# Reordering the products of a seven-product block multiplication in a mixture-of-experts layer: (1,2) before (0,3)

## Chip, cores, metric

One core of one Trainium2 chip. The metric is device time in microseconds (us) of one execution; lower is better.

## The reference

Attention (4 batches, 8 heads, 768 positions) makes `x` (3072 x 512). Then comes a mixture of 8 experts with fixed mixing weights `P`, 3072 x 8, from a Sinkhorn iteration:

```python
    for e in range(E):
        h = np.maximum(x @ w1[e], 0.0)
        ye = h @ w2[e]
        out += P[:, e:e + 1] * ye
```

The change touches `x @ w1[e]` of experts 1 to 7 only.

## The kernel before

Experts 1 to 7 work on six chunks of 512 tokens. Each (expert, chunk) of layer 1 is a 2 x 2 block product with seven products instead of eight, once per half `g` of the output columns: 14 products named `(g, k)`. I call one (expert, chunk) a **round**; the layer 1 of the very first one is plain, so there are 41 rounds. Layer 2 of the chunk before runs interleaved: a round has seven slots, each with two layer-1 products (4 matmuls each) and one layer-2 product (8 matmuls).

```python
        def copy(g, name, bank):          # ScalarE: PSUM -> SBUF, one buffer per name
            R[name] = mp.tile([128, 2, 256], F32, tag=f"R{name}", bufs=1, name=f"R{name}")
            nc.scalar.activation(out=R[name], in_=banks[g, bank], func=AF.Copy, bias=0.0, scale=1.0)
        ...
        def relu_sum(g, i, n, bank, name):   # VectorE: h = relu(bank + R[name])
            nc.vector._custom_dve(TENSOR_ADD_SAT, out=block(g, i, n), in0=banks[g, bank],
                                  in1=R[name], s0=65504.0, s1=0.0)

        def step(g, k):
            if k == 1:
                product(g, 1, "y", first=True)
                copy(g, "1", "y")
            if k == 2:
                product(g, 2, "z", first=True, last=True)
                relu_sum(g, 0, 0, "z", "1")
            if k == 6:
                product(g, 6, "y")
                copy(g, "2", "y")
            if k == 5:
                product(g, 5, "w", first=True)
                copy(g, "5", "w")
            if k == 7:
                product(g, 7, "y")
                relu_sum(g, 1, 1, "y", "5")
            if k == 3:
                product(g, 3, "w", last=True)
                relu_sum(g, 0, 1, "w", "2")
            ...                               # k == 4: product into y, relu on ScalarE

        for pair in (((0, 1), (0, 2)), ((0, 5), (0, 6)), ((0, 3), (1, 1)), ((0, 7), (1, 2)),
                     ((1, 5), (1, 6)), ((0, 4), (1, 7)), ((1, 3), (1, 4))):
            for g, k in pair:
                step(g, k)
            yield
```

The comments are added here. The banks y, z, w are PSUM banks out of a pool of four. Product (0,3) adds into w and so must wait until ScalarE has copied w after (0,5); (1,7) adds into y and must wait for the copy of y after (1,6).

The accumulators of expert 0 are weighted by `P` on ScalarE while expert 1 runs, 24 instructions in all.

```python
    def weight_first(c):
        for nb in range(4 * c, 4 * c + 4):
            nc.scalar.activation(out=acc_of(nb), in_=acc_of(nb), func=AF.Copy,
                                 bias=0.0, scale=Pne[:, nb, 0:1])
            yield
    ...
    def body(n):
        ...
        for slot in range(7):
            go("l1", 2 if n == 0 and slot == 0 else 1)
            if slot in (1, 5):
                go("w")
                go("x", 2)
            go("l2")
            if slot in (2, 3, 5, 6):
                go("first")
            ...
    with tc.manual_schedule(engines={mybir.EngineType.DVE}):
        for n in range(len(works)):
            body(n)
```

Part of layer 2 is added into the accumulators by an accumulating DMA from a tile `add` with three buffers. Only VectorE keeps the program's order; the scheduler orders the other engines, and it pulls the weightings of all six chunks into the first rounds.

The softmax here doesn't subtract the row's maximum and nothing guards it: scores larger than these inputs give would overflow.

## Time and profile before

| | |
|---|---|
| time, median of 3 runs | 700.89 us (700.46 to 701.01) |
| span of the profiled run | 699.1 us |
| first layer-1 product of round 1 to the end of the last matmul ("stage") | 184.31 to 694.995, 510.68 us |
| round 1, round 2 | 13.92, 12.83 us |
| every other round from 3 to 40 | 12.23 us |

A round's length is the distance between the starts of its product (0,1) and that of the next round in the timeline. Gaps below are distances between matmul starts less 0.109 us, the usual distance.

The page of before, engines' busy time and the chain that ended last:

```profile
PE 683.9 (98%) x6913; PEld 568.7 (81%) x6913; DVE 570.9 (82%) x1149; ACT 419.8 (60%) x775; POOL 151.4 (22%) x183
...
PE 92%; ACT 4%; DVE 2%; issue 1%; POOL 0%; ACTq 0%
```

The windows view of before: rounds 1 to 3 and one stretch of 100 us later. The first number after the window is its length, then each engine's busy time.

```profile
core 0: us, PE busy (x) PEld busy (x) DVE busy (x) ACT busy (x) POOL busy (x), PEclk, DMA share, GB/s
184.31:198.23 13.92, 12.58 (x114) 10.92 (x113) 10.93 (x22) 13.92 (x28) 1.30 (x2) 1.00 0.27 46
198.23:211.05 12.82, 12.58 (x114) 10.93 (x112) 11.88 (x24) 11.34 (x22) 2.59 (x4) 1.00 0.35 61
211.05:223.28 12.23, 12.23 (x115) 10.96 (x112) 12.04 (x25) 6.98 (x14) 2.54 (x4) 1.00 0.38 66
300.00:400.00 100.00, 100.00 (x918) 89.63 (x917) 86.83 (x160) 55.64 (x114) 22.77 (x27) 1.00 0.53 88
```

From round 3 to round 40, PE never stops. The Trainium skill, "Perfetto Trace Analysis", section "Identifying the Most-Contended Engine", warns that matmul busy time is not a good measure of the distance to the roofline; what shows saturation here is that the starts come every 0.109 us without a gap. In round 1 ScalarE is busy for all of the 13.92 us. In round 3 VectorE is busy 12.04 of 12.23 us.

The timeline of before in round 1 (start, duration, engine, line, operation, tiles, count, idle time and its releaser). Source line 718 is a layer-1 product, 727 the copies R, 733 the relu sums, 641 the weightings.

```profile
188.15 0.64 ACT L727 ACTIVATE R_3541<-l1w 128x512 f32<-128x512 f32 x1
188.63 0.65 ACT L727 ACTIVATE R_3547<-l1y 128x512 f32<-128x512 f32 x1
188.84 0.60 PE L718 MATMUL l1w<-xT_77,S_1_3450 128*128 128x256 f16 x4 [0.85 <-ACT R_3541 L727]
189.11 1.39 ACT L641 ACTIVATE acc_81<-acc_81,Pne 128x512 f32<-128x512 f32 x2
...
193.97 0.66 ACT L727 ACTIVATE R_3618<-l1w 128x512 f32<-128x512 f32 x1
...
194.45 0.67 ACT L727 ACTIVATE R_3624<-l1y 128x512 f32<-128x512 f32 x1
...
195.17 0.60 PE L718 MATMUL l1y<-T_1_3466,S_1_3450 128*128 128x256 f16 x4 [0.50 <-ACT R_3624 L727]
```

The product at 188.84 is (0,3): it waits for the copy of w, which stands behind weightings on ScalarE. The product at 195.17 is (1,7): it waits for the copy R2 of (1,6). By distances between starts the gaps are 1.01 and 0.66 us; the brackets are smaller (0.85 and 0.50) because a modelled matmul end lies later than the next start could. Round 2 has three gaps, of 0.12, 0.40 and 0.09 us, at 200.53, 202.24 and 208.00.

The timeline of before in round 3, which is typical of rounds 3 to 5:

```profile
218.28 0.68 DVE L733 CUSTOM_DVE_ANT_0 hT_3_3872<-l1y,R_3902 128x512 f16<-128x512 f32 x1
...
218.88 0.68 DVE L733 CUSTOM_DVE_ANT_0 hT_3_3872<-l1z,R_3935 128x512 f16<-128x512 f32 x1
...
219.08 0.60 ACT L727 ACTIVATE R_3980<-l1w 128x512 f32<-128x512 f32 x1
...
219.57 0.60 ACT L727 ACTIVATE R_3986<-l1y 128x512 f32<-128x512 f32 x1
...
220.22 0.60 PE L718 MATMUL l1y<-T_3_3730,S_1_3450 128*128 128x256 f16 x4
```

VectorE sums (0,7), then as the fourth of the round's six sums (1,2). ScalarE copies R5 and then R2 (219.57), and (1,7) follows at 220.22, 0.05 us after the copy's end, yet without a gap behind the product before it. So R2's copy has no slack in this round.

### The profile page before, as it was taken

The numbers are of one execution on the slowest core, as the hardware profiler recorded it, in microseconds if no ns is written. First come the engines' busy times: TensorE is split into PE (matmuls) and PEld (weight loads), VectorE is DVE, ScalarE is ACT, GpSimd is POOL, SyncE is SP. The second block draws the span as 40 slices with busy tenths as digits, with TensorE's granted clock in tenths as the row PEclk, the third lists the DMA queues.
The fourth block names the chain that finished last, engine by engine and source line by source line (L and its number), as shares of the span: only waits on it lengthen the run. The fifth ranks groups of instructions, "written<-read, shape, count | busy, mean of one in ns | idle before, by whom it ended". The sixth has DMA issues, their size and how long they took to land.

```text
span 699.1 us, 17004 instructions
## 1 busy us (share of the span) xinstructions
PE 683.9 (98%) x6913; PEld 568.7 (81%) x6913; DVE 570.9 (82%) x1149; ACT 419.8 (60%) x775; POOL 151.4 (22%) x183
## 2 busy tenths in 40 slices
PE   6999999999999999999999999999999999999997
PEld 3666666666588888888888888888888888888885
DVE  7785765757889988888888878988898788988785
ACT  6777676774896554655555565555556555555651
POOL 7432220000012131212212121122212212121210
PEclk8999999999999999999999999999999999999999
DMA  9999591000734287346824594349533964245776
GB/s 180 183 192 129 48 77 17 2 1 2 121 60 76 49 128 129 63 76 110 147 48 75 91 153 77 61 68 164 88 62 61 144 114 77 46 76 108 143 158 153
DMA packets 84256, 65.62 MB, mean 94 GB/s; under 512 B 48336, under 2 KB 64720, under 8 KB 84176
## 3 DMA queue, kind: packets, MB, share of 16 engines
q0 software_dynamic: 74976, 57.17, 58.5%
q1 hardware_dynamic: 7552, 6.30, 3.8%
q10 hardware_dynamic: 1648, 1.05, 0.6%
q8 instruction: 54, 0.88, 0.5%
q14 instruction: 26, 0.21, 0.1%
HBM read 52.45 MB, written 6.29 MB: 84 GB/s over the span
## 4 chain that ended last, share of the span: by engine, by line
PE 92%; ACT 4%; DVE 2%; issue 1%; POOL 0%; ACTq 0%
PE l1y L718 20%; PE l2y L783 20%; PE l1w L718 10%; PE l2w L783 10%; PE l1z L718 5%; PE l2z L783 5%; PE l1b L698 1%; ACT acc_81 L641 0%; PE l_3312 L375 0%; PE l_3246 L375 0%; PE l_1684 L375 0%; PE l_1568 L375 0%; ACT PT_1_0_0_318 L463 0%; PE last_10658 L835 0%; PE last_10646 L835 0%
## 5 line engine op out<-in xcount | busy, mean ns | idle before, releaser
L797 ACT ACTIVATE add<-l2z,Pne 128x256 f32<-128x256 f32 x80 | 33.6, 472 | 77.2 <-PE l2z L783 77.2
L797 ACT ACTIVATE add<-l2w,Pne 128x256 f32<-128x256 f32 x80 | 33.6, 472 | 28.3 <-PE l2w L783 26.5
L797 ACT ACTIVATE add<-l2y,Pne 128x256 f32<-128x256 f32 x80 | 33.7, 473 | 11.6 <-PE l2y L783 9.9
L361 PEld LDWEIGHTS <-w_0_124 128*128 128x128 f16 x384 | 35.4, 98 | 4.0 <-issue 0.2
L805 POOL DMA_DIRECT2D acc_79<-add x21 | 17.7, 844 | 78.4 <-ACT add L797 23.1
L805 POOL DMA_DIRECT2D acc_81<-add x21 | 17.7, 844 | 68.7 <-ACT add L797 29.2
L805 POOL DMA_DIRECT2D acc_80<-add x21 | 17.7, 845 | 67.6 <-ACT add L797 30.0
L805 POOL DMA_DIRECT2D acc_82<-add x21 | 17.8, 847 | 67.0 <-ACT add L797 31.0
L805 POOL DMA_DIRECT2D acc_83<-add x18 | 15.1, 841 | 54.2 <-ACT add L797 22.9
L805 POOL DMA_DIRECT2D acc_84<-add x18 | 15.4, 856 | 45.0 <-ACT add L797 31.8
L800 DVE SCALAR_TENSOR_TENSOR acc_83<-l2y,Pne,acc_83 128x256 f32<-128x256 f32 x44 | 19.2, 477 | 2.9 <-PE l2y L783 2.9
L800 DVE SCALAR_TENSOR_TENSOR acc_79<-l2y,Pne,acc_79 128x256 f32<-128x256 f32 x42 | 18.3, 478 | 3.1 <-PE l2y L783 3.0
L800 DVE SCALAR_TENSOR_TENSOR acc_82<-l2y,Pne,acc_82 128x256 f32<-128x256 f32 x42 | 18.3, 478 | 3.0 <-PE l2y L783 3.0
L800 DVE SCALAR_TENSOR_TENSOR acc_81<-l2y,Pne,acc_81 128x256 f32<-128x256 f32 x42 | 18.3, 477 | 3.0 <-PE l2y L783 3.0
L800 DVE SCALAR_TENSOR_TENSOR acc_80<-l2y,Pne,acc_80 128x256 f32<-128x256 f32 x42 | 18.3, 477 | 2.9 <-PE l2y L783 2.9
L718 PEld LDWEIGHTS <-S_5_6866 128*128 128x128 f16 x192 | 18.8, 98 | 2.2
L718 PEld LDWEIGHTS <-S_2_3728 128*128 128x128 f16 x192 | 18.8, 98 | 2.2
L718 PEld LDWEIGHTS <-S_6_7900 128*128 128x128 f16 x192 | 18.8, 98 | 2.2
L718 PEld LDWEIGHTS <-S_7_8934 128*128 128x128 f16 x192 | 18.8, 98 | 2.2
L718 PEld LDWEIGHTS <-S_3_4798 128*128 128x128 f16 x192 | 18.8, 98 | 2.2
L718 PEld LDWEIGHTS <-S_4_5832 128*128 128x128 f16 x192 | 18.8, 98 | 2.2
L718 PEld LDWEIGHTS <-S_1_3450 128*128 128x128 f16 x160 | 15.6, 98 | 4.1 <-issue 2.1
(2563 smaller groups left out, 2249.1 us busy)
## 6 DMA issues: line engine op xcount, KB each, us to landing
acc_79<-add POOLq DMA_DIRECT2D x21, 256.0 KB, 3.3
acc_80<-add POOLq DMA_DIRECT2D x21, 256.0 KB, 3.3
acc_81<-add POOLq DMA_DIRECT2D x21, 256.0 KB, 3.3
acc_82<-add POOLq DMA_DIRECT2D x21, 256.0 KB, 3.3
acc_83<-add POOLq DMA_DIRECT2D x18, 256.0 KB, 3.4
acc_84<-add POOLq DMA_DIRECT2D x18, 256.0 KB, 10.2
w_0_124<-in_moe_w_dram POOLq DMA_DIRECT2D x1, 1024.0 KB, 12.4
w_0_131<-in_moe_w_dram POOLq DMA_DIRECT2D x1, 1024.0 KB, 18.2
```

Of the source, the lines that this page charges most:

```text
L361: nc.tensor.matmul(out=l1[:, ts(fb % 2, 256)], lhsT=w1[:, dc, ts(fb, 128)], rhs=xT[dc // 2][:, dc % 2, c0:c0 + 256], start=(dc == 0), stop ...
L698: nc.tensor.matmul(out=l1, lhsT=w1[:, dc, ts(fb, 128)], rhs=xT[dc // 2][:, dc % 2, ts(c, CH)], start=(dc == 0), stop=(dc == 3),)
L718: nc.tensor.matmul(out=banks[g, bank][:, f, :], lhsT=lefts1[e][k - 1][:, dc, ts(2 * g + f, 128)], rhs=rights1[c][k - 1][:, dc, :], start=( ...
L783: nc.tensor.matmul(out=banks[bank][q], lhsT=lefts2[e, c][k - 1][:, q, f, :], rhs=rights2[e][k - 1][:, f, :], start=(first and q == 0 and f ...
L797: nc.scalar.activation(out=t[:, q, :], in_=banks[bank][q], func=AF.Copy, bias=0.0, scale=w)
L800: nc.vector.scalar_tensor_tensor(out=dst, in0=banks[bank][q], scalar=w, in1=dst, op0=ALU.mult, op1=ALU.add,)
L805: nc.gpsimd.dma_start(out=acc[c][:, i, n, :, :], in_=t, accum_op=ALU.add)
```

## The change

The intent: give the third slot to (1,1) and (1,2), which need nothing from ScalarE's late copies, and run (0,3) one slot later, when its operands for the sum have long been ready.

```diff
-        for pair in (((0, 1), (0, 2)), ((0, 5), (0, 6)), ((0, 3), (1, 1)), ((0, 7), (1, 2)),
+        for pair in (((0, 1), (0, 2)), ((0, 5), (0, 6)), ((1, 1), (1, 2)), ((0, 7), (0, 3)),
                      ((1, 5), (1, 6)), ((0, 4), (1, 7)), ((1, 3), (1, 4))):
```

The built programs have the same number of instructions on every engine; only their order and their waits differ.

## The prediction

> **What bounds the kernel now.** The page gives PE 683.9 of 699.1 us (98%); the chain that ended last is 92% PE. In the windows from 300 to 600 us PE is busy 100% at a granted clock of 1.00. A busy PE row proves little by itself, so I read starts: in the timeline of one (expert, chunk) round (406.68 to 418.90 us, 12.22 us) a group of 4 matmuls starts every 0.435 us and one of 8 every 0.87, about 109 ns per 256-column matmul. The Trainium skill, "TensorE: Matmul & The Clock Gate", section "Wait — 56ns, not 53.3ns?", gives N / 2.4 GHz + about 2.5 ns, which is 109.2 ns for N = 256; this trace agrees. In 39 of the 41 rounds of the transformed layers PE streams without a gap; no order of products makes that faster.
>
> Gaps exist only in the first two rounds: 1.01 us at 188.84 and 0.40 at 202.24, before product (0,3), which waits for ScalarE's copy of (0,5); 0.66 at 195.17 and 0.09 at 208.00, before (1,7), which waits for the copy of (1,6). About 2.2 us. There ScalarE is busy weighting the accumulators (0.7 us each).
>
> **What the change does.** Nothing is added or removed. In each round (0,3) moves from third to fourth slot, (1,2) from fourth to third; on VectorE their sums change places; ScalarE's copy of (1,1) comes about 0.44 us earlier. The PSUM bank of w stays open a slot longer, but the built program puts the second w into the bank that (1,2)'s sum has freed, at the same place in VectorE's order as before: that sum ends near 412.1, (1,5) starts at 413.67, so no new wait.
>
> **On the critical path.**
> 1. Round 1: (1,1) starts near 187.83, 1.01 us earlier than (0,3) did. But from 188.15 to 195.12 ScalarE works without a gap, on the same work in either order, and (1,7) waits for its last copy. I expect (1,7) at 195.17 as before: gain 0.
> 2. Round 2: 0.40 us gained at 202.24, lost again at (1,7), because VectorE runs back to back from 203.3 to 207.3.
> 3. New dependence: one R2 buffer. The copy of (1,6) must wait until (0,3)'s sum has read the old R2; that sum is now the fifth of the round. In rounds 2 to 5 the fifth sum ends 0.012 us before that copy starts; ScalarE starts about 0.11 us after the VectorE instruction it waits for (R5's copy: 206.74 to 206.86). So the copy comes 0.10 us later, and (1,7), 0.05 us behind it without slack, too: about +0.1 us a round, in 4 rounds: +0.4 us.
> 4. From round 6 on the distance is 0.28 us and (1,7) has 0.12 us of slack: nothing. Last round (distance 0.05): up to +0.06.
>
> Sum: 700.9 + 0.4 = **701.3 us**, 8 in 10 between 700.5 and 702.2. Faster by over 2%: 0.5%; within 2%: 98.5%; slower by over 2%: 1%.
>
> **What would show it.** The waits at 188.84 and 202.24 gone; (1,7) of round 1 still waiting on ScalarE near 195.2, of round 2 near 208.1; rounds 2 to 5 each about 0.1 us longer, from 6 on still 12.22 us.
>
> **What would make it wrong.** ScalarE's chain in round 1 getting shorter (gain up to 1 us); the 0.11 us not paid or absorbed (701.0); the R2 wait reaching the later rounds (0.1 us times 36: 705); bank reuse waiting for another sum than I read.

## The result, and the profile after

After: 701.01 us median of 4 runs (700.53 to 701.64); before, in the same rounds: 700.74 us (700.46 to 701.01). The ratio is 1.0004, 95% interval 0.9987 to 1.0022. A ratio here is the mean time of one kernel's runs over that of the other's in the same rounds, so not quite the ratio of the medians quoted. By time alone nothing can be told. The trace tells more: the stage went from 510.68 to 511.09 us (184.226 to 695.317), 0.41 us longer.

| round | 1 | 2 | 3 | 4 | 5 | 6 | 7 | 8 to 40, each |
|---|---|---|---|---|---|---|---|---|
| before | 13.92 | 12.83 | 12.23 | 12.23 | 12.23 | 12.23 | 12.23 | 12.23 |
| after | 13.90 | 12.92 | 12.32 | 12.32 | 12.33 | 12.23 | 12.27 | 12.23 |

The page of after:

```profile
PE 684.7 (98%) x6913; PEld 568.7 (81%) x6913; DVE 573.6 (82%) x1149; ACT 420.0 (60%) x775; POOL 151.4 (22%) x183
...
PE 91%; ACT 5%; DVE 3%; issue 1%; DMA 1%; ACTq 0%
```

The windows view of after, for the same rounds:

```profile
184.23:198.12 13.89, 12.72 (x113) 10.85 (x112) 10.92 (x22) 13.89 (x28) 1.30 (x2) 1.00 0.27 46
198.12:211.05 12.93, 12.51 (x115) 10.87 (x113) 11.88 (x24) 11.26 (x22) 2.60 (x4) 1.00 0.35 61
211.05:223.37 12.32, 12.32 (x115) 10.94 (x113) 12.03 (x25) 7.07 (x14) 2.54 (x4) 1.00 0.38 66
300.00:400.00 100.00, 100.00 (x918) 89.62 (x917) 87.58 (x159) 55.81 (x115) 22.76 (x27) 1.00 0.54 88
```

Round 3 is 0.09 us longer although PE still counts as busy in all of it: a wait of 0.1 us disappears in the modelled matmul ends. Only starts show it.

The timeline of after in round 1:

```profile
187.73 0.60 PE L718 MATMUL l1y<-xT_76,w_1_2386 128*128 128x256 f16 x4
...
188.05 0.64 ACT L727 ACTIVATE R_3541<-l1w 128x512 f32<-128x512 f32 x1
...
188.53 0.65 ACT L727 ACTIVATE R_3547<-l1y 128x512 f32<-128x512 f32 x1
...
193.87 0.66 ACT L727 ACTIVATE R_3618<-l1w 128x512 f32<-128x512 f32 x1
...
194.35 0.67 ACT L727 ACTIVATE R_3624<-l1y 128x512 f32<-128x512 f32 x1
...
195.07 0.60 PE L718 MATMUL l1y<-T_1_3466,S_1_3450 128*128 128x256 f16 x4 [1.16 <-ACT R_3624 L727]
```

This run's stage starts 0.08 us earlier, so its times are to be moved by that. The third slot now starts at 187.73 with (1,1), 1.1 us earlier than (0,3) did (1.03 us on before's time axis). But ScalarE's last copy starts at 194.35, where it was 194.45, and (1,7) at 195.07, where it was 195.17. The gap in front of (1,7) has grown from 0.66 to 1.32 us, and two new gaps of 0.17 us stand before layer-2 products, at 188.77 and 192.43; each of the two starts 0.05 to 0.06 us after the end of the VectorE instruction that it waits for. The growth and the two new gaps make 1.0 us: what was gained at (0,3) was paid back there.

The timeline of after in round 3:

```profile
218.27 0.68 DVE L733 CUSTOM_DVE_ANT_0 hT_3_3872<-l1y,R_3902 128x512 f16<-128x512 f32 x1
218.47 0.60 PE L718 MATMUL l1y<-T_3_3730,S_1_3450 128*128 128x256 f16 x4
...
218.87 0.68 DVE L733 CUSTOM_DVE_ANT_0 hT_3_3872<-l1w,R_3908 128x512 f16<-128x512 f32 x1
...
219.07 0.60 ACT L727 ACTIVATE R_3980<-l1w 128x512 f32<-128x512 f32 x1
...
219.67 0.60 ACT L727 ACTIVATE R_3986<-l1y 128x512 f32<-128x512 f32 x1
...
220.31 0.60 PE L718 MATMUL l1y<-T_3_3730,S_1_3450 128*128 128x256 f16 x4
```

The fourth sum is now (0,3)'s, and it reads the old R2 (R_3908) until 219.55. The copy into the same buffer (R_3986) starts 0.116 us after that end, at 219.67 instead of 219.57, and (1,7) moves from 220.22 to 220.31.

### The profile page after: what moved, and what is told of

Its sections match the earlier page's. It is cut to its first block, busy times and chain, and to the rows that moved or that the text cites. A ratio compares the mean times of both kernels' runs of the same rounds, so it can differ in the third digit from the quotient of the medians.

```text
span 699.4 us, 16963 instructions
## 1 busy us (share of the span) xinstructions
PE 684.7 (98%) x6913; PEld 568.7 (81%) x6913; DVE 573.6 (82%) x1149; ACT 420.0 (60%) x775; POOL 151.4 (22%) x183
## 4 chain that ended last, share of the span: by engine, by line
PE 91%; ACT 5%; DVE 3%; issue 1%; DMA 1%; ACTq 0%
PE l1y L718 20%; PE l2y L783 20%; PE l2w L783 10%; PE l1w L718 10%; PE l1z L718 5%; PE l2z L783 5%; PE l1b L698 1%; DMA ret_u<-in_is_retrieval_dram 1%; DVE acc_80 L800 0%; ACT acc_81 L641 0%; ACT acc_82 L641 0%; ACT add L797 0%; DVE hT_2_3690 L733 0%; PE l_3312 L375 0%; PE l_3246 L375 0%
```

## The experiments

Two theories were on trial. Theory A: ScalarE's backlog of weightings fixes when (1,7) can start in round 1, so closing the gap at (0,3) gains nothing. Theory B: the loss of 0.1 us a round in rounds 2 to 5 is the wait for the one R2 buffer. The main rivals: the order itself costs or gains (PSUM banks, places of sums), or a closed gap is a gain that stays.

| run | time, median (range) of 5 | before, same rounds | ratio (95%) | rounds 1, 2, 3, 4, 5 | stage |
|---|---|---|---|---|---|
| after_r2x2 | 700.86 (700.41 to 701.17) | 700.84 | 1.0000 (0.9986 to 1.0013) | 13.92, 12.82, 12.23, 12.23, 12.23 | 510.70 |
| after_r25x2 | 700.31 (699.70 to 700.72) | 700.84 | 0.9991 (0.9978 to 1.0003) | 13.91, 12.46, 12.23, 12.23, 12.23 | 510.42 |
| before_swap | 700.61 (700.05 to 701.86) | 700.84 | 0.9999 (0.9986 to 1.0012) | 13.91, 12.82, 12.23, 12.23, 12.23 | 510.69 |
| new_order_e_over_1 | 700.66 (700.10 to 701.25) | 700.84 | 0.9998 (0.9986 to 1.0011) | 13.91, 12.82, 12.23, 12.23, 12.23 | 511.16 |
| before_unweighted | 698.91 (698.81 to 699.37) | 700.82 | 0.9974 (0.9962 to 0.9987) | 12.34, 12.23, 12.23, 12.23, 12.23 | 508.51 |
| after_unweighted | 700.18 (699.62 to 700.47) | 700.82 | 0.9990 (0.9977 to 1.0002) | 12.46, 12.23, 12.32, 12.60, 12.33 | 509.68 |
| before_program_order | 700.99 (700.95 to 701.22) | 700.82 | 1.0003 (0.9991 to 1.0016) | 12.68, 12.80, 12.80, 12.80, 12.80 | 511.22 |
| after_program_order | 701.14 (700.71 to 701.71) | 700.82 | 1.0007 (0.9993 to 1.0021) | 12.69, 12.80, 12.80, 12.81, 12.80 | 511.25 |
| before_r25x2 | 700.53 (699.95 to 700.65) | 700.74 | 0.9996 (0.9984 to 1.0009) | 13.90, 12.73, 12.23, 12.23, 12.23 | 510.58 |
| best_old_order | 698.30 (697.94 to 698.54) | 700.74 | 0.9966 (0.9952 to 0.9980) | 12.43, 12.23, 12.23, 12.23, 12.23 | 508.60 |
| best_new_order | 698.49 (698.02 to 698.81) | 700.74 | 0.9968 (0.9956 to 0.9981) | 12.43, 12.23, 12.23, 12.23, 12.23 | 508.60 |

Rounds 8 to 40 together took 403.48 us in before and after and in all of these runs but two, which are told below. No interval of time but those of before_unweighted and the two best versions excludes 1; where smaller effects are judged it is by the trace, one profile for each kernel.

### after_r2x2

```diff
-            R[name] = mp.tile([128, 2, 256], F32, tag=f"R{name}", bufs=1, name=f"R{name}")
+            R[name] = mp.tile([128, 2, 256], F32, tag=f"R{name}", bufs=1 + (name in ("2",)), name=f"R{name}")
```

> The changed kernel with two R2 buffers instead of one; the order of instructions on every engine is that of the changed kernel. Length of a round = from the start of its product (0,1) to that of the next round. Theory (the copy of (1,6) waits until the late sum of (0,3) has read the one R2 buffer): rounds 2 to 5 go back from 12.92, 12.32, 12.32, 12.33 to 12.83, 12.23, 12.23, 12.23 us as in the kernel before, because R5's copy just ahead still waits for VectorE; the transformed stage falls from 511.09 to 510.7 us, the time by 0.4 us. Rival (the 0.1 us a round comes from the order itself: PSUM banks or the sums' places on VectorE): rounds 2 to 5 stay 0.1 us longer than before, stage 511.1.

The order of instructions is that of after on every engine; only the wait went. Rounds 2 to 5 came back to 12.82 and 12.23, the stage to 510.70. The timeline in round 2 (tile numbers are missing in this trace; the second sum shown is (0,3)'s, the two copies are R5 and R2):

```profile
206.69 0.68 DVE L733 CUSTOM_DVE_ANT_0 hT<-l1w,R 128x512 f16<-128x512 f32 x1
...
206.89 0.60 ACT L727 ACTIVATE R<-l1w 128x512 f32<-128x512 f32 x1 [0.48 <-DVE hT L733]
...
207.38 0.59 ACT L727 ACTIVATE R<-l1y 128x512 f32<-128x512 f32 x1
...
208.02 0.60 PE L718 MATMUL l1y<-T,S 128*128 128x256 f16 x4 [0.31 <-ACT R L727]
```

R2's copy starts at 207.38, 0.01 us after the sum's end (207.37), and no longer 0.116 us after it. Theory B holds, its rival falls. The copy of R5 ahead of it still waits for VectorE, so (1,7) still has no slack.

### after_r25x2

The same edit with `("2", "5")`.

> The changed kernel with two buffers each for R2 and R5. Theory: neither copy in front of (1,7) waits for VectorE any more; the stall at (1,7) of round 2 (0.58 us) goes for the most part, rounds 3 to 5 go to 12.23, round 2 to 12.3 to 12.6 us; round 1 stays 13.9, since there ScalarE's own queue is the limit; the stage comes to 510.1 to 510.5 us, 0.2 to 0.6 under the kernel before. Rival (VectorE is so loaded in rounds 2 to 5 that its next result stops PE instead): round 2 stays at 12.8, stage 510.7. Rival 2 (order itself costs): as in the run with R2 alone, stage 511.1.

The timeline in round 2, R5's copy, R2's copy, (1,7):

```profile
205.98 0.60 ACT L727 ACTIVATE R<-l1w 128x512 f32<-128x512 f32 x1
...
206.46 0.61 ACT L727 ACTIVATE R<-l1y 128x512 f32<-128x512 f32 x1
...
207.24 0.60 PE L718 MATMUL l1y<-T,S 128*128 128x256 f16 x4
```

The copies now come straight behind ScalarE's adds, and (1,7) stands 0.44 us behind (0,4) at 206.80, without a gap. Round 2 fell to 12.46. The stage, 510.42, lies in the range expected; 0.11 us of it is a single gap at 555 us, told below.

### before_swap

```diff
-((0, 3), (1, 1))
+((1, 1), (0, 3))
```

> The kernel before with only (1,1) and (0,3) exchanged inside the third slot; sums keep their places on VectorE, so no new wait for R2. Theory: the gap in front of (0,3) shrinks from 1.01 to about 0.57 us in round 1 and from 0.40 to 0 in round 2, and (1,7) of round 1 still starts when ScalarE's last copy is done, so round 1 stays 13.9 and round 2 12.8, all others 12.23: stage 510.7, time as before. Rival (a gap closed at (0,3) is a gain that stays): stage 0.4 to 0.8 us shorter, 509.9 to 510.3.

The timeline in round 1, (0,3) and (1,7):

```profile
188.89 0.60 PE L718 MATMUL l1w<-xT,S 128*128 128x256 f16 x4 [0.41 <-ACT R L727]
...
195.22 0.60 PE L718 MATMUL l1y<-T,S 128*128 128x256 f16 x4 [0.94 <-ACT R L727]
```

The gap at (0,3) shrank from 1.01 to 0.57 us and that at (1,7) grew from 0.66 to 1.10. Round 1 stayed 13.91. A gap closed early in a round whose last copy is late is not a gain: theory A.

### new_order_e_over_1

```diff
-        for pair in (((0, 1), (0, 2)), ((0, 5), (0, 6)), ((0, 3), (1, 1)), ((0, 7), (1, 2)),
+        third, fourth = ((((1, 1), (1, 2)), ((0, 7), (0, 3))) if e > 1 else
+                         (((0, 3), (1, 1)), ((0, 7), (1, 2))))
+        for pair in (((0, 1), (0, 2)), ((0, 5), (0, 6)), third, fourth,
```

> The new order only from the second transformed expert on (rounds 6 to 41), the old order in rounds 1 to 5. Theory: rounds 1 to 5 as before (13.92, 12.83, 12.23 x3), rounds 6 to 41 12.227 us each: stage 510.7, time 700.7 to 701.0, ratio 1.000. Rival (the new order costs or gains something small in each round, also where the trace shows slack): 36 rounds times 0.01 us or more would show in their lengths.

Rounds 1 to 5 were as before, and the new order was 12.226 to 12.227 us in every round from 6 to 40 but one. So where there is slack, the order itself costs nothing in these rounds. The stage missed my number by 0.46 us, because of a single gap of 0.49 us in front of a product (0,6) at 555.9 us:

```profile
554.53 0.84 ACT L799 ACTIVATE add<-l2y,Pne 128x256 f32<-128x256 f32 x2 [1.37 <-DMA acc<-add]
...
555.91 0.60 PE L718 MATMUL l1y<-T,S 128*128 128x256 f16 x4 [0.33 <-ACT R L727]
```

There ScalarE's add stood still for 1.37 us until an accumulating DMA had landed and freed a buffer of `add`; the copy behind it, R1, came late. Before's trace has the same kind of wait at the same place, 0.39 us long, which stops nothing. Such a wait, 0.02 to 0.5 us of PE in a round in which the weights of a coming expert are loaded, was seen in five other traces (in round 7: after 0.04, after_r2x2 and before_swap 0.02, after_unweighted 0.48; in round 31: after_r25x2 0.11). I take it for chance in the landing of DMAs and part of the scatter of the times: in round 7 of before the same wait is 0.88 us long and stops nothing, in after it is 0.93 and costs 0.04. But no experiment tested that, and the four losses over 0.03 us all came with the new order, in four of its six traces with three buffers of `add`, against none of five of the old order. That the order has a part in it is not excluded.

### before_unweighted and after_unweighted

Wrong results (relative error 2.2): 20 of the 24 weightings are left out, in the kernel before and in the changed one.

```diff
-            gens["first"] = weight_first(c)
+            gens["first"] = weight_first(c) if c == 0 else iter(())
```

> Wrong result on purpose: the kernel before without 20 of the 24 ScalarE instructions that weight the accumulators (only those of the first chunk stay), so that ScalarE's queue has no backlog in rounds 1 and 2. Theory (the two waits of (0,3) and the waits of (1,7) there come from that backlog): all four gaps go, rounds 1 to 5 are 12.23 to 12.3 us, stage 508.3 to 508.7 us, 2.0 to 2.3 under before, with the old order. Rival (the waits at (0,3) come from the order, not from the backlog): gaps stay in front of (0,3) in round 1.

> Wrong result on purpose: the same removal in the changed kernel. Theory: with the backlog gone the new order has nothing to gain, and only the wait for the R2 buffer is left: rounds 2 to 5, perhaps round 1, are 12.32 where before_unweighted has 12.23: stage 0.4 to 0.5 us longer than before_unweighted. Rival (the new order does gain at (0,3), hidden only by the backlog): stage equal to before_unweighted or shorter.

The timeline of before_unweighted in round 1, (0,3) and (1,7):

```profile
187.27 0.60 PE L718 MATMUL l1w<-xT,S 128*128 128x256 f16 x4
...
193.07 0.60 PE L718 MATMUL l1y<-T,S 128*128 128x256 f16 x4
```

(0,3) follows the product before it without a gap, and 0.12 us is left at (1,7). With the backlog gone and the **old** order, rounds 1 and 2 take 12.34 and 12.23: nearly all of the 2.2 us of gaps was ScalarE's backlog, not the order. The stage fell by 2.17 us. That settles theory A. The new order is longer here, by 0.12 in round 1, 0.09 in round 3 and 0.10 in round 5, each at (1,7); in round 2 it is not longer, against my expectation: (1,7) starts at 205.97 there, exactly one group of 0.44 us behind (0,4), so the R2 wait fits. The stage was expected 0.4 to 0.5 us longer and came out 1.16 us longer. Two parts of that are not the wait that was expected: 0.48 us is the DMA wait told above, and in round 4 R2's copy started 0.39 us after the sum's end instead of 0.116, which no record explains. That 0.28 us stays open. The rest, 0.41 us, is what was expected. The times show a loss over 0.41 us too: the means of the two kernels' five runs differ by 1.08 us, and their ranges do not overlap. So part of the other 0.76 us may recur in every run, and chance is not shown as its cause.

### before_program_order and after_program_order

```diff
-    with tc.manual_schedule(engines={mybir.EngineType.DVE}):
+    with tc.manual_schedule(engines={mybir.EngineType.DVE, mybir.EngineType.Activation}):
```

> Correct result: the kernel before with ScalarE kept in program order in the transformed layers, so that the weighting is spread over six rounds, four instructions each, instead of being pulled into rounds 0 to 2. The build also moves (1,7) into the middle of the layer-2 product behind it in rounds 1 to 5. Theory: gaps at (0,3) and (1,7) go for the most part, rounds 1 and 2 come to 12.23 to 12.5 us, stage 508.4 to 509.2, time 0.2 to 0.3% under before. Rival (rounds 1 and 2 are held by VectorE too): round 2 stays over 12.6.

> Correct result: the same in the changed kernel. Since (1,7) stands 0.4 us later here, the wait of 0.1 us for the R2 buffer should be hidden: rounds 1 to 5 within 0.05 us of before_program_order, stage within 0.2 us of it. Rival (the new order helps once ScalarE keeps up): stage shorter than before_program_order by 0.3 us or more.

The first expectation was wrong: round 1 fell by 1.23 us, but rounds 2 to 5 rose to 12.80, and the stage was 511.22. The timeline at the start of round 3 of before_program_order shows why:

```profile
210.41 0.74 ACT L641 ACTIVATE acc<-acc,Pne 128x512 f32<-128x512 f32 x1
...
211.02 0.62 ACT L727 ACTIVATE R<-l1y 128x512 f32<-128x512 f32 x1
...
211.67 0.69 DVE L733 CUSTOM_DVE_ANT_0 hT<-l1z,R 128x512 f16<-128x512 f32 x1 [0.37 <-ACT R L727]
...
219.16 0.28 PE L783 MATMUL l2w<-w,S 128*128 128x256 f16 x1 [0.31 <-DVE S L655]
```

One weighting now stands ahead of R1's copy, the first of the round. VectorE waits 0.37 us for it, and since VectorE works back to back from then on, from 211.67 to 219.10, it does not catch up until PE stops: 0.48 us by the starts at the layer-2 product behind (0,4), at 219.16, which waits for VectorE's operand. So the rival was right: VectorE holds these rounds as soon as its chain starts late. Between old and new order there is 0.03 us in the stage, as expected.

### before_r25x2

> The kernel before, old order, with two buffers each for R2 and R5: is the 0.37 us that after_r25x2 gained in round 2 a gain of the buffers alone or of the new order once the buffers let it through? Theory (new order's gain at (0,3), let through): here (0,3) of round 2 still waits 0.40 us for ScalarE, only the 0.09 us before (1,7) go: round 2 is 12.73 (12.46 in after_r25x2), round 1 13.9, the rest 12.23: stage 510.6. Rival (buffers alone): round 2 is 12.46 here too, stage 510.3.

The buffers alone bring round 2 to 12.73, the new order with the buffers to 12.46. So in round 2 the new order does have a worth of 0.27 us, once the copies in front of (1,7) do not wait for VectorE. In the change as it was made, the single buffers took that gain back.

### best_old_order and best_new_order

```diff
-bufs=1, name=f"R{name}")
+bufs=1 + (name in ("2", "5")), name=f"R{name}")
...
-                t = mp.tile([128, 2, 256], F32, tag="add", bufs=3, name="add")
+                t = mp.tile([128, 2, 256], F32, tag="add", bufs=5, name="add")
...
+            if slot in (1, 3, 5):
+                go("first", 1 + (slot == 3))
             go("l2")
-            if slot in (2, 3, 5, 6):
-                go("first")
...
-    with tc.manual_schedule(engines={mybir.EngineType.DVE}):
+    with tc.manual_schedule(engines={mybir.EngineType.DVE, mybir.EngineType.PE, mybir.EngineType.Activation}):
```

> Correct result: old order; TensorE, VectorE and ScalarE in program order; the four weighting instructions of a round put where ScalarE was idle in the trace (one behind the copies of the second slot, two ahead of the adds of the fourth, one ahead of those of the sixth); two buffers for R2 and R5, five for the tile that the accumulating DMA reads. Theory (rounds 1 and 2 are held by ScalarE's backlog alone; before_program_order lost because a weighting stood ahead of the copies that start VectorE's chain): rounds 1 to 5 within 12.23 to 12.4, stage 508.3 to 509.0, time 698.4 to 699.2. Rival (with weighting spread, ScalarE is late again somewhere): rounds 1 to 5 at 12.5 or more, stage over 510.

> The same with the new order. Theory: with no backlog and two R2 buffers the order neither gains nor loses: rounds 1 to 5 within 0.05 us of best_old_order, stage within 0.15 us. Rival (the new order has a worth of its own): stage shorter by 0.3 us or more.

The windows view of best_old_order, rounds 1 to 3:

```profile
183.85:196.28 12.43, 12.43 (x113) 10.78 (x112) 10.74 (x22) 9.96 (x19) 1.37 (x2) 1.00 0.32 55
196.28:208.51 12.23, 12.23 (x115) 10.96 (x112) 11.92 (x24) 9.31 (x18) 2.50 (x4) 1.00 0.37 64
208.51:220.74 12.23, 12.23 (x115) 10.96 (x113) 12.05 (x25) 9.31 (x18) 2.52 (x4) 1.00 0.38 66
```

ScalarE's work in round 1 is 9.96 us instead of 13.92, because the weightings are spread. Both versions give correct results and 698.3 and 698.5 us, ratios 0.9966 and 0.9968, the fastest kernels, faster than before and after by some 0.3%. The two orders have the same rounds to 0.01 us: with the two causes gone, the order of the pairs is worth nothing here. Which of the edits carries how much was not taken apart.

## Why the prediction was right

- **Bound.** 39 of 41 rounds of before have no gap on PE (but for 0.02 us in round 41), and the new order left the untroubled rounds at 12.227 us. Right. An estimate from the Trainium skill, "TensorE: Matmul & The Clock Gate", section "Wait — 56ns, not 53.3ns?" (N / 2.4 GHz + about 2.5 ns for back-to-back matmuls), is 109.2 ns for 256 columns; the 0.109 us here agrees. The prediction's list of gaps left out one of 0.12 us in round 2, at 200.53; it is 0.11 us after the change, so this did no harm.
- **Round 1: gain 0.** 13.92 became 13.90. Right; before_swap and before_unweighted show the cause, the backlog on ScalarE. The two gaps of 0.17 us before layer-2 products were not foreseen; they cost nothing, since (1,7) waits for ScalarE's last copy anyway.
- **Round 2: 0.40 us gained and lost again.** 12.83 became 12.92, which is the loss and the 0.1 us of the next point. (1,7) at 207.99, or 208.07 on before's time axis, 208.1 predicted. Right, and after_r25x2 against before_r25x2 shows that the gain was there and was held back by the buffers.
- **R2 buffer: +0.1 us a round in rounds 2 to 5, 0.4 in all.** Measured +0.10, +0.09, +0.09, +0.10, sum 0.39; the wait of 0.11 us was 0.116. after_r2x2, which takes only this wait away, takes back all of it. The section "Optimization Strategy" of the Trainium skill's "Perfetto Trace Analysis" says that the same gap repeating over a stretch on the engine that should be saturated can mean too few buffers; here that was so, with one buffer of R2 and a gap of 0.1 us in four rounds.
- **Rounds from 6 on: nothing.** Right but for 0.04 us in round 7, which stands behind the DMA wait told above. The fourth sum ends 0.28 us before the copy there, more than the 0.116 us it needs.
- **Last round: up to +0.06.** Nothing showed: from the start of round 41 to the last matmul's end it is 19.33 us before and after. The copy starts 0.116 us after the sum's end there too, instead of 0.053, but (1,7) starts only 0.34 us after that copy has ended.
- **Size.** +0.41 us in the stage; +0.27 us between the medians, less than the scatter of the runs, so the time alone would not have confirmed it. 701.3 was predicted, 701.01 measured.

## What to carry to other kernels

Before reordering work to close a gap, find the last wait of the round: if another engine's queue is full up to it, a gap closed earlier only moves there. A new order also changes which read of a single buffer comes last; look at each one-buffer tile for a writer that now waits for a later reader, and measure its slack against the hand-over time between the engines. And put extra work into an engine's idle stretches, not ahead of the first copy of a chain that another, nearly full engine works off; before_program_order against best_old_order points to this, though more than that differs between the two.

## What the Trainium skill lacked or had wrong

- No page that I read gives the time from the end of an instruction on one compute engine to the start of one that waits for it on another; "Perfetto Trace Analysis" draws the step in which a semaphore update spreads, but puts no figure to it. In these traces: VectorE to ScalarE 0.116 us (rounds 2 to 5 of after), ScalarE to PE 0.051 us ((1,7) behind R2's copy), ScalarE to VectorE 0.03 us (the second sum of a round behind the second half's R1 copy, rounds 6 and later of after). It would belong to "Perfetto Trace Analysis".
- "Perfetto Trace Analysis", "Identifying the Most-Contended Engine", rightly warns against matmul busy time, but does not say that short waits vanish in it; the page tells in its section "Tensor Engine Instruction (MATMUL, LD_WEIGHTS)" that a matmul's end is an estimate, but not this consequence: round 3 of after is 12.32 us with PE busy 12.32 us, and has a wait of 0.1 us that only the starts show.
- "ScalarE: Activation LUTs", "What ACT_TABLE_LOAD costs", says that back-to-back ACTIVATEs overlap by about 93 ns. The trace is near it and a little above: in best_old_order two copies of 0.60 us in round 1 start 0.49 us apart (186.233 and 186.727), an overlap of 0.10 us, and the R5 and R2 copies ahead of (1,7) overlap by 0.12 us (median of rounds 6 to 41).
